# Inverse DFT over m written interleaved over four r, and a second buffer for x1s

## The chip, the cores and the metric

The kernel runs on one core of a Trainium2 chip. The metric is the device time of one execution in microseconds; lower is better. Before the change three runs took 784.08, 786.80 and 788.09 us, median 786.8.

## The reference

The computation has two parts. The first is a gated recurrence over time, the second a "Hyena" operator: a projection to three tensors, a long circular convolution of the second one through FFTs, a product of all three, and an output projection. Shapes: batch B = 4, time S = 6272, width D = 256, all float32.

```python
# first part: recurrence over t
sig = 1.0 / (1.0 + np.exp(-f_logit))
f = lower_bound + (1.0 - lower_bound) * sig
h = f[:, t] * h + (1.0 - f[:, t]) * x[:, t]        # for t in range(S); x becomes all h
# second part
proj = x @ w_proj                                   # (B, S, 3 D)
x1, x2, x3 = proj[..., :D], proj[..., D:2 * D], proj[..., 2 * D:]
X2 = np.fft.rfft(x2, n=S, axis=1)
H = np.fft.rfft(filter_fft, n=S, axis=0)[None]
x2_conv = np.fft.irfft(X2 * H, n=S, axis=1)
y = x1 * x2_conv * x3
return y @ w_out
```

## The kernel before

Time is split as t = 49 m + r with m from 0 to 127 and r from 0 to 48 (in the code Q = 49, M = 128), so that an FFT of length 6272 = 128 x 49 becomes matmuls over m and over r. One batch after the other goes through these phases:

- `hgrn(b)`: the recurrence, in 13 chunks of 512 time steps. A chunk loads x and f_logit, transposes them on TensorE (L146, L148), runs the scan on VectorE (L153), and computes x1 and x3 with float32 matmuls (L164). ScalarE copies x1 from PSUM into the tile `x1s` (L167), and VectorE multiplies x3 from PSUM with it into `z` = x1 * x3, float16 (L168). This runs twice per chunk, for jb = 0 and 1, the halves of the 256 channels. `x1s` has one buffer here, by `bufs=1`; the pool's own number is two. The scan's result also goes to `HA` for the later phases.
- `phase_p(b)`: projects x2 with weights read from `HA` at a step of 49 elements (L379) and evicts four r at a time into `x2` (L383 on VectorE, L385 on ScalarE), in runs of four float16.
- `phase_f1(b)`: the DFT over m (L394).
- `mini(b)` (L408 to L418) and `units(b)`: the DFT over r (L435), the product with the filter's spectrum (L439), the inverse over r (L447), evicted into `Th` (L450). `units(b)` is woven with `hgrn(b + 1)`.
- `phase_o(b)`: the inverse DFT over m, the gate and the output projection. It is the phase that the diff rewrites.

`phase_o` walks over r in 13 steps: twelve of four r and one with r = 48 alone. A step of four r has these instructions:

- L468, 16 matmuls on TensorE, each 64 contraction rows by 128 columns of m: for each r, two terms (`rr`) that accumulate, and two halves p of the channels, which use different 64 partitions of `Th` and write different PSUM banks. The result `pc` holds, for each p, four blocks of 128 m, one block per r.
- L473, one product on VectorE over 1024 elements per partition: `y` = `pc` * `z`, with y in float16 in the buffer `PP`. `z` lies in the order of time, so for a fixed r its elements over m are 49 elements (98 bytes) apart.
- L481, 16 matmuls on TensorE with y as the weights (128 x 128) and `w_out` as the moving operand (256 columns). `w_out` is split into a high and a low float16 part, `Woh` and `Wol`, and each weight tile is loaded for both.
- L485 evicts the result from PSUM to `osb` on ScalarE, and L486 stores it. `osb` has two buffers.

PSUM is one tile of eight banks, handed out in four pairs by `pair()`; `pc` takes one pair and the projection's result the next. The tile framework's scheduler sets the order of the instructions on each engine and adds the waits. On TensorE it puts two steps of `phase_o` together: 32 L468, then 32 L481, and so on, six times, and the single r = 48 at the end. The order on an engine is fixed when the program is built.

Of the kernel before, what the change touches and what calls it, by code (L numbers as in the profile page):

```python
# [9 lines left out]
F32 = mybir.dt.float32  # L10
# [3 lines left out]
AOP = mybir.AluOpType  # L14
# [10 lines left out]
Q = 49  # L25
TB = 98
CH = 512
# [17 lines left out]
def m0_of(r):  # L45
    return (128 * q_of(r) - r) // Q
# [22 lines left out]
def kernel(  # L69
# [10 lines left out]
    nc = tc.nc  # L80
# [32 lines left out]
    hg = ctx.enter_context(tc.tile_pool(name="hg", bufs=2))  # L113
    dram = ctx.enter_context(tc.tile_pool(name="dram", bufs=1, space=bass.MemoryType.DRAM))
    H = [dram.tile([TB, 2, UE * 64], F16, name=f"H{u}") for u in range(NU)]
    zt = [konst.tile([128, 2, S], F16, name="z0"), None]
# [4 lines left out]
    def pair():  # L121

        turn[0] = (turn[0] + 1) % turn[1]
        return PS[:, 2 * turn[0]:2 * turn[0] + 2]


    def hgrn(b):
        z = zt[b % 2]
        last = [None, None]
        for c in range(NCHK):  # L130
            t0 = c * CH
            nb = min(CH, S - t0) // 128
            n = nb * 128
            xt = hg.tile([128, 4, D], F32, name="xt", tag="xt", bufs=3)
            nc.sync.dma_start(xt[:, 0:nb], x[b, t0:t0 + n, :].rearrange("(j p) d -> p j d", p=128))
            ft = hg.tile([128, 4, D], F32, name="ft", tag="ft", bufs=3)
            nc.sync.dma_start(ft[:, 0:nb], f_logit[b, t0:t0 + n, :]
                              .rearrange("(j p) d -> p j d", p=128))
            nc.scalar.activation(ft[:, 0:nb], ft[:, 0:nb], AF.Sigmoid, scale=-1.0)  # L139
            nc.gpsimd.tensor_tensor(xt[:, 0:nb], xt[:, 0:nb], ft[:, 0:nb], op=AOP.mult)  # L140
            for kh in range(2):
                cols = slice(kh * 128, kh * 128 + 128)
                sT = PS[:, 6, 0:n]
                uT = PS[:, 7, 0:n]
                for j in range(nb):
                    nc.tensor.transpose(sT[:, j * 128:(j + 1) * 128], ft[:, j, cols], iden[:])  # L146
                for j in range(nb):
                    nc.tensor.transpose(uT[:, j * 128:(j + 1) * 128], xt[:, j, cols], iden[:])  # L148
                fT = hg.tile([128, CH], F32, name="fT", tag="fT")
                nc.scalar.activation(fT[:, 0:n], sT, AF.Identity,  # L150
                                     scale=nomc[:, kh:kh + 1], bias=1.0)
                h = hg.tile([128, CH], F32R, name="h", tag=f"h{kh}")
                nc.vector.tensor_tensor_scan(  # L153
                    h[:, 0:n], fT[:, 0:n], uT,
                    0.0 if c == 0 else last[kh][:, CH - 1:CH].bitcast(F32),
                    op0=AOP.mult, op1=AOP.add)
                last[kh] = h
                nc.gpsimd.tensor_copy(HA[:, HB[kh] + t0:HB[kh] + t0 + n],  # L158
                                      h[:, 0:n].bitcast(F32))
            for jb in range(2):  # L160
                for i in range(2):
                    js = slice(i * 256 + jb * 128, i * 256 + jb * 128 + 128)
                    for kh in range(2):
                        nc.tensor.matmul(PS[:, 4 + i, 0:n], W13[:, kh, js], last[kh][:, 0:n],  # L164
                                         start=(kh == 0), stop=(kh == 1))
                x1s = hg.tile([128, CH], F32, name="x1s", tag="x1s", bufs=1)
                nc.scalar.activation(x1s[:, 0:n], PS[:, 4, 0:n], AF.Copy, scale=ZS)  # L167
                nc.vector.tensor_tensor(z[:, jb, t0:t0 + n], PS[:, 5, 0:n], x1s[:, 0:n],  # L168
                                        op=AOP.mult)
            yield  # L170
# [282 lines left out]

    def phase_o(b):
        Th = st["Th"]
        z = zt[b % 2][:].rearrange("p k (m r) -> p k r m", r=Q)
        tf = Th[:].rearrange("p c g -> p (c g)")
        for r0 in range(0, Q, 4):
            rn = min(4, Q - r0)
            pc = pair()  # L460
            for i in range(rn):
                r = r0 + i
                sh = (128 - m0_of(r)) % 128
                for rr in range(2):
                    c0 = (rr * Q + r) * 128
                    for p in range(2):
                        ps = slice(64 * p, 64 * p + 64)
                        nc.tensor.matmul(pc[:, p, i * 128:(i + 1) * 128], tf[ps, c0:c0 + 128],  # L468
                                         ID[ps, rr, sh:sh + 128],
                                         start=(rr == 0), stop=(rr == 1))  # L470
            y = PP[:, r0 // 4 % 4 // 2, r0 // 4 % 2].rearrange(
                "p a i k -> p a (i k)").rearrange("p a (i m) -> p a i m", m=128)[:, :, 0:rn]
            nc.vector.tensor_tensor(  # L473
                y, pc[:, :, 0:rn * 128].rearrange("p a (i m) -> p a i m", m=128),
                z[:, :, r0:r0 + rn, :], op=AOP.mult)
            po = pair().rearrange("m a (q e) -> m (a q) e", e=256)
            for i in range(rn):
                n = 0
                for kh in range(2):
                    for w in (Woh, Wol):  # L480
                        nc.tensor.matmul(po[:, i, :], y[:, kh, i, :], w[:, kh, :],  # L481
                                         start=(n == 0), stop=(n == 3))
                        n += 1
            osb = cw.tile([128, 4, 256], F32, name="osb", tag="osb")
            nc.scalar.activation(osb[:, 0:rn, :], po[:, 0:rn, :], AF.Copy, scale=OS)  # L485
            nc.sync.dma_start(out[b].rearrange("(a r) d -> a r d", r=Q)[:, r0:r0 + rn, :],  # L486
                              osb[:, 0:rn, :])
            yield

    with tc.tile_pool(name="tmp", bufs=1) as tmp:  # L490
        prep = prepare(tmp)
        next(prep)
        weave((hgrn(0), NCHK), (prep, 1 + 13 + NU + 1))
# [6 lines left out]
    PP = cv.tile([128, 2, 2, 2, UE, 64], F16, name="PP")  # L500
    run(phase_p(0))
    run(phase_f1(0))
    for b in range(B):
        mini(b)
        if b + 1 < B:
            weave((units(b), NU), (hgrn(b + 1), NCHK))
        else:
            run(units(b))
        if b + 1 < B:
            wraps()  # L510
        run(phase_o(b))
        if b + 1 < B:
            run(phase_p(b + 1))
            run(phase_f1(b + 1))
# [30 lines left out]
```

## Time and profile before

| | |
|---|---|
| median of three runs | 786.8 us (784.08 to 788.09) |
| profiled execution, its own time | 786.94 us |
| its span | 785.2 us |
| mean granted TensorE clock | 0.954 |
| PE busy | 645.1 us (82%) |
| DVE busy | 567.9 us (72%) |
| ACT busy | 390.1 us (50%) |
| POOL busy | 198.4 us (25%) |
| HBM | 128 GB/s over the span |

PE is TensorE's matmuls, PEld its weight loads, DVE is VectorE, ACT ScalarE, POOL GpSimd, and SP issues the DMAs. A matmul's length in the profile includes its own pipeline, so matmuls overlap, and a busy PE isn't a PE at its peak. A group's line reads: line, engine, operation, output<-inputs, shapes, count, busy us, mean ns of one, idle time of the engine before them and what ended it. Line numbers are those of the kernel before, and the same in the kernel after.

### The profile page before, as it was taken

To read this page: it belongs to the slowest core of one execution; us is meant where nothing else is said; L and a number is where in the kernel's file an instruction comes from. 1 tells how busy PE (TensorE), PEld (TensorE's weight loads), DVE (VectorE), ACT (ScalarE), POOL (GpSimd) and SP (SyncE) were. 2 spreads that over 40 slices of the span, in tenths; PEclk is the share of its full clock that TensorE was granted. 3 is DMA by queue.
4 is the path that set the end of the run, shared out by engine and by line. 5 is a ranking of instruction groups with operands and counts; after the bars stand their busy time and mean duration, and the time that the engine had idled before them with its cause. 6 is when DMAs were issued, how large, how long until landed. Compare 5 with 4: busy or idle time off the path is not lost.

```text
span 785.2 us, 13221 instructions
## 1 busy us (share of the span) xinstructions
PE 645.1 (82%) x5252; PEld 483.2 (62%) x5252; DVE 567.9 (72%) x574; ACT 390.1 (50%) x495; POOL 198.4 (25%) x264
## 2 busy tenths in 40 slices
PE   4698897689999867889898766899999867989775
PEld 3576666575666555766665555766666656857554
DVE  6996464288888765697888566698898665889564
ACT  3697666475655423665455423665555223823232
POOL 2446434104454310005434400015443000001000
PEclk9899998899999989999999989999999999989899
DMA  9765546205664733224665723124663233012133
GB/s 326 242 213 153 184 128 203 97 1 174 193 186 156 256 127 134 88 66 137 196 191 158 236 108 153 70 70 149 213 194 122 89 148 157 13 51 83 59 140 141
DMA packets 73630, 113.99 MB, mean 145 GB/s; under 512 B 4416, under 2 KB 55488, under 8 KB 72800
## 3 DMA queue, kind: packets, MB, share of 16 engines
q1 hardware_dynamic: 73568, 113.15, 42.9%
q8 instruction: 41, 0.67, 0.4%
q14 instruction: 21, 0.17, 0.1%
HBM read 71.70 MB, written 28.90 MB: 128 GB/s over the span
## 4 chain that ended last, share of the span: by engine, by line
PE 36%; DVE 22%; issue 13%; ACT 8%; DMA 8%; POOL 0%; DVEq 0%; ACTq 0%; SPq 0%; POOLq 0%
PE PS L481 8%; DVE PP L473 8%; PE PS L164 7%; DVE h L153 7%; PE PS L379 5%; PE PS L447 5%; DVE PP L439 5%; DMA ft<-in_f_logit_dram 4%; DMA Hu<-H 4%; PE PS L468 2%; PE PS L394 2%; PE PS L148 2%; PE PS L346 2%; PE PS L435 2%; ACT x1s L167 1%
## 5 line engine op out<-in xcount | busy, mean ns | idle before, releaser
L473 DVE TENSOR_TENSOR PP<-PS,z 128x1024 f16<-128x1024 f32 (+1 forms) x52 | 113.4, 2220 | 76.0 <-PE PS L468 56.4
L164 PE MATMUL PS<-h,W 128*128 128x512 f32 (+1 forms) x416 | 148.9, 443 | 17.5 <-DVE h L153 10.7
L439 DVE TENSOR_TENSOR PP<-PS,Hu 98x1008 f16<-98x1008 f32 x128 | 151.2, 1194 | 9.6 <-PE PS L435 3.4
L481 PE MATMUL PS<-Woh,PP 128*128 128x256 f16 x392 | 101.8, 299 | 54.0 <-DVE PP L473 53.7
L140 POOL TENSOR_TENSOR xt<-xt,ft 128x1024 f32<-128x1024 f32 (+1 forms) x52 | 116.6, 2243 | 101.7 <-DMA xt<-in_x_dram 54.8
L153 DVE TENSOR_TENSOR_SCAN h<-fT,h,PS 128x512 fp32r<-128x512 f32 (+1 forms) x96 | 116.0, 1208 | 23.4 <-ACT fT L150 7.9
L481 PEld LDWEIGHTS <-PP 128*128 128x128 f16 x784 | 79.7, 106 | 78.9 <-DVE PP L473 63.4
L485 ACT ACTIVATE osb<-PS 128x1024 f32<-128x1024 f32 (+1 forms) x52 | 50.7, 975 | 139.6 <-PE PS L481 139.6
L168 DVE TENSOR_TENSOR z<-PS,x1s 128x512 f16<-128x512 f32 (+1 forms) x104 | 68.3, 657 | 59.2 <-ACT x1s L167 37.2
L447 PEld LDWEIGHTS <-PP 98*128 98x128 f16 x1024 | 84.7, 99 | 38.5 <-issue 28.2
L158 POOL CAST HA<-h 128x512 f16<-128x512 f32 (+1 forms) x104 | 61.6, 594 | 170.8 <-DVE h L153 167.6
L481 PE MATMUL PS<-Wol,PP 128*128 128x256 f16 x392 | 101.1, 297 | 0.0
L447 PE MATMUL PS<-VB,PP 98*128 98x196 f16 x512 | 95.6, 250 | 0.3
L164 PEld LDWEIGHTS PS<-h,W 128*128 128x128 f32 x416 | 66.2, 195 | 43.7 <-DVE h L153 24.6
L167 ACT ACTIVATE x1s<-PS 128x512 f32<-128x512 f32 (+1 forms) x104 | 59.3, 571 | 66.6 <-PE PS L164 62.9
L450 ACT CAST Th<-PS 128x784 f16<-128x784 f32 x64 | 51.9, 811 | 71.6 <-PE PS L447 71.5
L150 ACT ACTIVATE fT<-PS,nomc 128x512 f32<-128x512 f32 (+1 forms) x104 | 69.0, 663 | 33.8 <-PE PS L146 29.6
L435 PE MATMUL PS<-HA,FT 98*128 98x512 f16 x256 | 77.7, 386 | 4.6 <-DVE PP L439 2.8
L148 PE MATMUL PS<-iden,xt 128*128 128x128 f32 x392 | 67.9, 283 | 11.2 <-DVE h L153 10.2
L146 PE MATMUL PS<-iden,ft 128*128 128x128 f32 x392 | 70.2, 279 | 3.8 <-ACT fT L150 3.2
L139 ACT ACTIVATE ft<-ft 128x1024 f32<-128x1024 f32 (+1 forms) x52 | 52.4, 1008 | 29.7 <-DMA ft<-in_f_logit_dram 25.0
L447 PE MATMUL PS<-VA,PP 98*128 98x196 f16 x256 | 61.0, 250 | 4.5 <-ACT Th L450 2.5
(112 smaller groups left out, 792.3 us busy)
## 6 DMA issues: line engine op xcount, KB each, us to landing
xt<-in_x_dram SPq DMA_DIRECT2D x48, 512.0 KB
ft<-in_f_logit_dram SPq DMA_DIRECT2D x48, 512.0 KB
out_dram<-osb SPq DMA_DIRECT2D x48, 512.0 KB
Hu<-H SPq DMA_DIRECT2D x64, 196.0 KB
HA<-in_moe_filter_fft_dram SPq DMA_DIRECT2D x6, 1024.0 KB
HA<-HA SPq DMA_DIRECT2D x12, 512.0 KB
H<-HA SPq DMA_DIRECT2D x16, 196.0 KB
HA<-HA SPq DMA_DIRECT2D x4, 544.0 KB
```

Of the source, the lines that this page charges most:

```text
L140: nc.gpsimd.tensor_tensor(xt[:, 0:nb], xt[:, 0:nb], ft[:, 0:nb], op=AOP.mult)
L146: nc.tensor.transpose(sT[:, j * 128:(j + 1) * 128], ft[:, j, cols], iden[:])
L148: nc.tensor.transpose(uT[:, j * 128:(j + 1) * 128], xt[:, j, cols], iden[:])
L150: nc.scalar.activation(fT[:, 0:n], sT, AF.Identity, scale=nomc[:, kh:kh + 1], bias=1.0)
L153: nc.vector.tensor_tensor_scan(h[:, 0:n], fT[:, 0:n], uT, 0.0 if c == 0 else last[kh][:, CH - 1:CH].bitcast(F32), op0=AOP.mult, op1=AOP.add)
L164: nc.tensor.matmul(PS[:, 4 + i, 0:n], W13[:, kh, js], last[kh][:, 0:n], start=(kh == 0), stop=(kh == 1))
L168: nc.vector.tensor_tensor(z[:, jb, t0:t0 + n], PS[:, 5, 0:n], x1s[:, 0:n], op=AOP.mult)
L435: nc.tensor.matmul(PS[:, o, :], FT[:TB, tb, :], A[:TB, es, r, :], start=(n == 0), stop=(n == 1))
L439: nc.vector.tensor_tensor(P[:TB, o, :, :, 1:64], px.unsqueeze(1).broadcast_to([TB, 2, UE, 63]), hh, op=AOP.mult)
L447: nc.tensor.matmul(o, P[:TB, a, h, 2 * pr:2 * pr + 2, :], v[:TB], start=(n == 0), stop=(n == 3))
L473: nc.vector.tensor_tensor(y, pc[:, :, 0:rn * 128].rearrange("p a (i m) -> p a i m", m=128), z[:, :, r0:r0 + rn, :], op=AOP.mult)
L481: nc.tensor.matmul(po[:, i, :], y[:, kh, i, :], w[:, kh, :], start=(n == 0), stop=(n == 3))
```

## The change

Two edits. First, in `hgrn` the tile `x1s` gets the pool's two buffers instead of one. Second, in `phase_o` the order of the two inner indices m and i (the r within a step) is exchanged in `pc` and `y`: a matmul of L468 now writes every fourth word of its bank, so that the four r of one m lie side by side. L473 then reads `pc` and writes `y` in that order, and reads `z` in runs of four neighbours, a run every 49 elements. L481 takes the weights of one r out of `y` at a step of four elements. The number and the sizes of the instructions stay. For the last step (r = 48, rn = 1) nothing changes.

```diff
-                x1s = hg.tile([128, CH], F32, name="x1s", tag="x1s", bufs=1)
+                x1s = hg.tile([128, CH], F32, name="x1s", tag="x1s")
...
-        z = zt[b % 2][:].rearrange("p k (m r) -> p k r m", r=Q)
+        z = zt[b % 2][:].rearrange("p k (m r) -> p k m r", r=Q)
...
-                        nc.tensor.matmul(pc[:, p, i * 128:(i + 1) * 128], tf[ps, c0:c0 + 128],
+                        nc.tensor.matmul(pc[:, p, i:i + rn * 127 + 1:rn], tf[ps, c0:c0 + 128],
                                          ID[ps, rr, sh:sh + 128],
                                          start=(rr == 0), stop=(rr == 1))
-            y = PP[:, r0 // 4 % 4 // 2, r0 // 4 % 2].rearrange(
-                "p a i k -> p a (i k)").rearrange("p a (i m) -> p a i m", m=128)[:, :, 0:rn]
+            y = PP[:, r0 // 4 % 4 // 2, r0 // 4 % 2].rearrange("p a i k -> p a (i k)")
+            y = y[:, :, 0:rn * 128].rearrange("p a (m i) -> p a m i", i=rn)
             nc.vector.tensor_tensor(
-                y, pc[:, :, 0:rn * 128].rearrange("p a (i m) -> p a i m", m=128),
-                z[:, :, r0:r0 + rn, :], op=AOP.mult)
+                y, pc[:, :, 0:rn * 128].rearrange("p a (m i) -> p a m i", i=rn),
+                z[:, :, :, r0:r0 + rn], op=AOP.mult)
...
-                        nc.tensor.matmul(po[:, i, :], y[:, kh, i, :], w[:, kh, :],
+                        nc.tensor.matmul(po[:, i, :], y[:, kh, :, i], w[:, kh, :],
```

The second buffer of `x1s` changes the order in which the scheduler places instructions, in the setup (one exchange on ScalarE) and in the first weave, where `units` of batch 0 stands with `hgrn` of batch 1. On ScalarE (ACT), a place in that weave read before as follows; `fT` is the scan's factor, `ft` the gate's input, `Th` the output of `units`, and the bracket names the engines that an instruction waits for.

```order
L167 ACTIVATE x1s_1717<-PS_104 128x512 [waits PE_49]
L150 ACTIVATE fT_1767<-PS_104,nomc_66 128x512 [waits DVE_49,PE_49]
L139 ACTIVATE ft_1925<-ft_1925 128x1024 [waits DMAHW1_49]
L167 ACTIVATE x1s_1724<-PS_104 128x512 [waits DVE_49,PE_49]
L150 ACTIVATE fT_1780<-PS_104,nomc_66 128x512 [waits PE_49]
L450 CAST Th_1510<-PS_104 128x196x4 [waits PE_49]
```

In the changed kernel the same place on ScalarE reads:

```order
L167 ACTIVATE x1s_1717<-PS_104 128x512 [waits PE_49]
L150 ACTIVATE fT_1767<-PS_104,nomc_66 128x512 [waits DVE_49,PE_49]
L167 ACTIVATE x1s_1724<-PS_104 128x512 [waits PE_49]
L139 ACTIVATE ft_1925<-ft_1925 128x1024 [waits DMAHW1_49]
L150 ACTIVATE fT_1780<-PS_104,nomc_66 128x512 [waits DVE_49,PE_49]
L450 CAST Th_1510<-PS_104 128x196x4 [waits PE_49]
```

The second copy of x1 (`x1s_1724`) no longer waits for VectorE, and stands ahead of the sigmoid of a coming chunk (`ft_1925`).

On TensorE (PE) the first difference lies in the same weave, where L435 and L447 belong to `units` and L148 and L164 to `hgrn`:

```order
 L447 LDWEIGHTS PP
 L447 MATMUL PS<-VN,PP 128x196
+L435 LDWEIGHTS FT
+L435 MATMUL PS<-HA,FT 128x512
 L148 MATMUL PS<-iden,xt 128x128 x4
 L164 MATMUL PS<-h,W_73 128x512 x2
```

A matmul of `units` moves ahead of the transposes and projections of `hgrn`. The order of the two later weaves, of `phase_o` and of the phases between them is the same before and after on every engine.

## The prediction

> **What bounds the kernel now.** I read the page first, for the chain of work that ended last.
>
> ```profile
> span 785.2 us, 13221 instructions
> PE 36%; DVE 22%; issue 13%; ACT 8%; DMA 8%; POOL 0%; DVEq 0%; ACTq 0%; SPq 0%; POOLq 0%
> PE PS L481 8%; DVE PP L473 8%; PE PS L164 7%; DVE h L153 7%; PE PS L379 5%; PE PS L447 5%; DVE PP L439 5%; DMA ft<-in_f_logit_dram 4%; DMA Hu<-H 4%; PE PS L468 2%; PE PS L394 2%; PE PS L148 2%; PE PS L346 2%; PE PS L435 2%; ACT x1s L167 1%
> ```
>
> Three lines of `phase_o` (L481, L473, L468) hold about 18% of the chain, beside part of the "issue" share. Next, the busy time by stage for the four passes of `phase_o`; the columns are the stretch, its length, then busy time (instructions) of PE, PEld, DVE, ACT and POOL, granted clock, DMA share and GB/s.
>
> ```profile
> 275.50:321.70 46.20, 32.37 (x369) 25.12 (x368) 28.42 (x14) 12.30 (x12) 2.61 (x2) 0.91 0.32 128
> 450.80:498.00 47.20, 34.16 (x382) 26.20 (x379) 28.32 (x14) 12.30 (x12) 0.25 (x1) 0.89 0.31 125
> 619.70:666.00 46.30, 32.96 (x381) 25.51 (x381) 28.35 (x14) 12.30 (x12) 0.25 (x1) 0.93 0.31 127
> 735.00:785.20 50.20, 33.01 (x378) 25.24 (x372) 28.35 (x13) 12.68 (x13) 0.00 (x0) 0.90 0.32 129
> ```
>
> Together 189.9 us, and no engine is full: PE 33 of 47, DVE 28 of 47. So they take turns. The timeline of one period shows how: start, length, engine and line, and in brackets the idle time before.
>
> ```profile
> 466.41 1.07 PE L468 MATMUL PS<-ID,Th 64*128 64x128 f16 x32
> 466.56 1.02 ACT L485 ACTIVATE osb<-PS 128x1024 f32<-128x1024 f32 x1 [1.23 <-PE PS L481]
> 467.07 4.59 DVE L473 TENSOR_TENSOR PP<-PS,z 128x1024 f16<-128x1024 f32 x2 [2.58 <-PE PS L468]
> ...
> 469.47 1.64 PEld L481 LDWEIGHTS <-PP 128*128 128x128 f16 x16 [2.16 <-DVE PP L473]
> 469.47 0.28 PE L481 MATMUL PS<-Woh,PP 128*128 128x256 f16 x1 [1.99 <-DVE PP L473]
> ...
> 471.72 1.64 PEld L481 LDWEIGHTS <-PP 128*128 128x128 f16 x16 [0.61 <-DVE PP L473]
> ...
> 473.57 0.62 PE L468 MATMUL PS<-ID,Th 64*128 64x128 f16 x16
> ```
>
> One period is two steps of four r: 32 inverse-DFT matmuls (L468), two gate products on DVE (L473), two groups of 16 projection matmuls (L481). It lasts 473.57 - 466.41 = 7.16 us, and its path is 0.66 (first half of L468 until DVE starts) + 4.59 (both gate products) + 0.06 (hand-over, 471.72 against 471.66) + 1.85 (second L481 group until the next L468). TensorE stands idle for 2.16 + 0.61 us waiting for L473, so the gate sets the pace. Its price and the nearest rows, by shape:
>
> ```profile
> L473 DVE TENSOR_TENSOR PP<-PS,z 128x1024 f16<-128x1024 f32 x48 | 110.5, 2345 | 65.9 <-PE PS L468 46.3 <-issue 19.5
> L439 DVE TENSOR_TENSOR PP<-PS,Hu 98x1008 f16<-98x1008 f32 x128 | 151.2, 1194 | 9.6 <-PE PS L435 3.4 <-DMA Hu<-H 2.8 <-PE PS L447 2.3
> L383 DVE CAST x<-PS 128x1024 f16<-128x1024 f32 x24 | 34.6, 1440 | 21.9 <-PE PS L379 21.9
> L341 DVE CAST af<-PS 98x1024 fp32r<-98x1024 f32 x8 | 9.8, 1223 | 7.5 <-PE PS L334 7.5
> L325 DVE CAST f<-PS 128x1024 fp32r<-128x1024 f32 x6 | 7.4, 1233 | 0.6 <-PE PS L321 0.6
> ```
>
> L473 and L439 are the same operation on nearly as many elements; L439 reads runs of 63 and takes 1194 ns, L473 reads z one element in every 49 (98 bytes) and takes 2345. The step costs 1.1 ns per element.
>
> **The change, part by part.**
>
> *The gate reads z in runs of four.* 48 instructions. Without any price for runs it would come to L439's rate, 1024/1008 x 1194 = 1213 ns; if each run of four paid the step's 1.1 ns twice, 1213 + 256 x 2.2 = 1776. In between lies L383, which writes runs of four f16 at the same 98-byte step into x2: 1440 ns. That is the same geometry, so I take 1.44, that is 0.9 us off each L473. The four last steps of a pass (r = 48 alone) read z one by one as before: no gain.
>
> *What the shorter gate is worth.* In the period, the first gate product now ends at 0.66 + 1.44 = 2.10, the first L481 group starts at 2.16. A group starts its 16 matmuls 109 ns apart, from the chain of waits:
>
> ```profile
> 471.72 1.92 PE PS L481 x16
> ```
>
> (1.92 - 0.28 of the last one's own length)/15 = 0.109, so 1.75 us for a group. The second product ends at 0.66 + 2.88 = 3.54, before the first group is through at 3.91: it is hidden, and TensorE is late next. Period: 0.66 + 1.44 + 0.06 + 1.75 + 1.85 = 5.76, against 7.16: 1.40 saved. ACT's eviction of 1.02 us per step and the stores (DMA share 0.31 to 0.32 in the passes above) leave room.
>
> *The inverse DFT writes every fourth word of PSUM.* 768 of the 784 L468 matmuls.
>
> ```profile
> L468 PE MATMUL PS<-ID,Th 64*128 64x128 f16 x784 | 30.1, 225 | 7.4 <-ACT Th L450 6.0 <-ACT x1s L167 1.4
> ```
>
> 32 of them take 1.07 us and one about 0.22, so they start (1.07 - 0.22)/31 = 27.5 ns apart, since the two halves of 64 partitions run side by side: 55 ns per pair of 128 columns. No matmul of the trace writes PSUM with a step, so I bound it. Nothing: L325 and L341 are one copy with and without a 1 KB step between the words that it reads from PSUM, 1233 and 1223 ns. Much: L408 reads its moving operand at a 256-byte step.
>
> ```profile
> L408 PE MATMUL PS<-HA,FT 98*128 98x256 f16 x8 | 4.1, 601 | 0.4 <-DVE HA L398 0.4
> L379 PEld LDWEIGHTS <-HA 128*128 128x128 f16 x392 | 44.2, 144 | 8.1 <-DMA HA<-HA 5.4 <-issue 0.8
> L394 PEld LDWEIGHTS <-x 128*128 128x128 f16 x512 | 29.5, 98 | 10.9 <-ACT x L385 7.4 <-issue 2.4
> ```
>
> It takes 601 ns against 280 (the L481 of the timeline) for 256 columns, 1.25 ns more per column, so 160 ns per pair and 1.28 us per step. The stepped accesses of the trace cost a factor of 1.0 (L325), 1.45 (L379's weights at 98 bytes), 1.95 (L473) and 4 (L408, 321 more on 109 ns). I take 2, the factor of L473, whose step is also one element out of each neighbourhood: 55 ns more per pair, 8 x 55 = 0.45 us per step. Only the first step's share is on the path (the second runs under the first gate product, 1.97 against 2.55 us), so a period is 5.76 + 0.45 = 6.21.
>
> The Trainium skill ("PSUM — Partial Sum Buffer", Specifications) says that PSUM has 8-byte lines and that any access pattern that isn't contiguous slows matmuls significantly. By it, one fp32 per line instead of two is an estimate of half the write rate, 0.45 us per step and 761 us in all; by the row L325, whose step costs 10 ns in 1024, it would be 750. No run so far shows a stepped write.
>
> *The projection loads its weights at a step of four.* 768 loads. Between 98 ns (L394, no step) and 144 (L379, 98 bytes): up to 46 more, under the 109 ns from matmul to matmul, which covers it. Only a period's first load has no cover: 24 x 23 ns (the middle) = 0.5 us.
>
> *x1s gets a second buffer.* The waits that it can remove, with total, count and longest, and the wait around it:
>
> ```profile
> ACT x1s L167 <- DVE z L168: 3.8, 5, 1.5
> DVE z L168 <- ACT x1s L167: 37.2, 30, 5.0
> ```
>
> ACT waits 3.8 us for z's readers in all, and that is the ceiling. The 37.2 us stay: z still waits for its own x1s. After a product over jb = 0, L164 must refill bank 5 before the next product, so ACT's earlier copy mostly waits there instead. I take 1.0 us. The order changes only in the setup (one swap on ACT) and in the first weave (units of batch 0 with hgrn of batch 1); the two later weaves and all of `phase_o` stand as before. For the new order I allow the size of that ceiling, 4 us, either way, and nothing in the mean.
>
> *The clock.* Per pass, the first period and one later are longer.
>
> ```profile
> 290.08:298.41 8.33, 6.33 (x65) 4.65 (x64) 4.62 (x2) 2.05 (x2) 0.00 (x0) 0.80 0.37 153
> 466.41:473.57 7.16, 4.84 (x65) 3.87 (x64) 4.59 (x2) 2.05 (x2) 0.00 (x0) 1.00 0.35 145
> 185.00:272.00 87.00, 79.88 (x545) 55.39 (x542) 73.47 (x75) 47.33 (x71) 39.81 (x46) 1.00 0.58 185
> ...
> 734.27:743.01 8.74, 7.11 (x64) 5.39 (x64) 4.60 (x2) 1.02 (x1) 0.00 (x0) 0.61 0.01 2
> ```
>
> The granted clock falls there, to a mean of 0.80 in a later period and 0.61 in a first one. In the weave, with PE busy 92%, it is 1.00. A period now has TensorE waiting for 2.8 us of 7.16, then for 0.6 of 6.21 (L468 done at 1.97, L481 from 2.61), so I expect the later drop to vanish: those four periods come from 8.33 to 6.21. In a first period PE is behind the gate once the clock is down, so only the first product counts: 0.90 - 0.45 = 0.45.
>
> *The sum.* 24 periods: 16 x (7.16 - 6.21) = 15.2; 4 x (8.33 - 6.21) = 8.5; 4 x 0.45 = 1.8; x1s 1.0; weights -0.5. In all 26.0 us off the profiled execution's 786.94 (its span 785.2): 760.9. The median of the three runs, 786.8, is 0.1 lower, so 761.
>
> **The rivals.**
>
> *Stepped PSUM writes cost nothing.* For it: L325. Then 16 x 1.40 + 4 x (8.33 - 5.76) + 4 x 0.90 + 0.5 = 36.8, giving 750.
>
> *The inverse DFT becomes the bound.* The other side. At L408's price 32 L468 last 1.07 + 2.56 = 3.63, and both gate products hide under PE. The period is L468 + 1.75 + 1.85 = 7.23; it equals 7.16 at 1.245 us per step (156 ns more per pair, nearly four times as slow), and from there on the kernel gets slower. At 1.28 a usual period is 0.07 longer. If the clock drops stay, a period of 8.33 spends 8.33 - 0.66 - 2.35 - 0.06 = 5.26 from the first L481 on, and becomes 3.63 + 5.26 = 8.89, for eight periods 0.56 longer: 16 x 0.07 + 8 x 0.56 = 5.6, giving 793. Against it: a step of 16 bytes is smaller than L408's 256.
>
> *Runs of four aren't faster to read.* L383 shows runs on the write side only. With L473 at 2.35 and the writes at a factor of two, each period is 0.45 longer: 797. Against it: L473's price goes with its step, since L439 has none.
>
> *The clock still drops.* Four periods at 0.45 instead of 2.11: 768, inside the first case.
>
> **How the numbers follow.** About 0.5% (4 us) is what a measurement of this kernel tells from no change. My case with or without clock drops 0.50; free writes 0.28; the inverse DFT as the bound 0.10; runs no faster 0.06; the rest, 0.06, is a gain eaten in part by the first weave or by something that no row shows. Faster 0.82, same 0.08, slower 0.10. The range starts at 745 (free writes with a gate of 1213 ns: 750 - 24 x 0.23) and reaches 778 (768, plus 16 x 0.34 for a gate of 1776 ns, plus 4 for the order); both slower rivals stay outside, 0.16 in all.
>
> **What would show each step.** L473 near 1440 ns, and TensorE's idle time before L481 falling from 2.2 us to under 1; a period of 6.2 us; 32 L468 in 2.0 us instead of 1.07 (1.07 means free writes, 3.6 the bound); L481's loads at most 144 ns and its matmuls still 109 ns apart; no clock below 1.00 after a pass's first period; ACT's 3.8 us wait for L168 gone, the first weave within 4 us of before. I am wrong if L468's matmuls lie more than 100 ns apart, if L473 stays above 2 us, or if L481's matmuls move apart.

## The result and the profile after

The changed kernel takes 757.8 us (median of four runs, 752.8 to 762.2) against 787.4 before (the three runs and a fourth): the ratio is 0.9625, with a 95% interval from 0.9554 to 0.9696. The forecast was 761 us. The profiled execution took 752.78 us with a span of 751.1, so it lies 5 us under the median; the four runs go only roughly with their mean granted clock (752.78 us at 0.973, 756.37 at 0.956, 759.15 at 0.962, 762.17 at 0.951).

The chain of work that ended last, from the page of the changed kernel:

```profile
PE 45%; DVE 24%; issue 11%; ACT 10%; DMA 9%; POOL 1%; DVEq 0%; SPq 0%; ACTq 0%
PE PS L481 11%; PE PS L164 9%; DVE h L153 8%; PE PS L447 5%; PE PS L379 5%; DMA ft<-in_f_logit_dram 5%; DVE PP L439 4%; DVE PP L473 4%; PE PS L468 3%; PE PS L148 2%; DMA Hu<-H 2%; PE PS L435 2%; PE PS L346 2%; PE PS L394 2%; ACT x1s L167 2%
```

The gate (L473) has gone from 8% to 4%, and the TensorE lines beside it (L481, L468) carry more. The four passes of `phase_o`, by stage, with the columns as before:

```profile
278.66:315.47 36.81, 34.40 (x377) 30.98 (x374) 14.96 (x14) 12.32 (x12) 0.24 (x1) 0.98 0.39 158
444.11:480.73 36.62, 33.74 (x382) 30.53 (x379) 14.89 (x14) 12.32 (x12) 1.02 (x2) 1.00 0.41 165
602.71:639.34 36.63, 33.74 (x382) 30.52 (x379) 14.90 (x14) 12.32 (x12) 0.25 (x1) 1.00 0.39 159
710.91:751.10 40.19, 32.99 (x376) 29.67 (x370) 14.84 (x13) 12.71 (x13) 0.00 (x0) 1.00 0.40 161
```

They sum to 150.3 us, where before it was 189.8 (the passes cut at the same events): 39.5 us gained. DVE's busy time in a pass is halved, PE is nearly full, and the clock is at 0.98 to 1.00, where it was 0.89 to 0.93. The span became 34.1 us shorter, so 5.4 us were lost outside the passes. One usual period in the timeline:

```profile
461.04 1.92 PE L468 MATMUL PS<-ID,Th 64*128 64x128 f16 x32
461.19 1.02 ACT L485 ACTIVATE osb<-PS 128x1024 f32<-128x1024 f32 x1 [0.72 <-PE PS L481]
462.13 2.36 DVE L473 TENSOR_TENSOR PP<-PS,z 128x1024 f16<-128x1024 f32 x2 [3.63 <-PE PS L468]
...
463.41 3.42 PEld L481 LDWEIGHTS <-PP 128*128 128x128 f16 x32 [0.73 <-DVE PP L473]
463.41 0.30 PE L481 MATMUL PS<-Woh,PP 128*128 128x256 f16 x1 [0.45 <-DVE PP L473]
...
467.03 1.92 PE L468 MATMUL PS<-ID,Th 64*128 64x128 f16 x32
```

It lasts 5.99 us: 1.09 until the gate starts, 1.22 for the first product, 0.06 to hand over, and 3.62 for both L481 groups, which now follow each other without a wait. TensorE waits once, for 0.45 us. The groups by shape:

```profile
L473 DVE TENSOR_TENSOR PP<-PS,z 128x1024 f16<-128x1024 f32 x48 | 56.6, 1220 | 80.3 <-PE PS L468 65.1 <-issue 15.2
L468 PE MATMUL PS<-ID,Th 64*128 64x128 f16 x784 | 50.6, 313 | 7.1 <-ACT Th L450 7.1
L481 PEld LDWEIGHTS <-PP 128*128 128x128 f16 x784 | 83.4, 114 | 19.7 <-DVE PP L473 18.4
```

The gate is down from 2345 to 1220 ns. A matmul of the inverse DFT is up from 225 to 313 ns, and 32 of them take 1.92 us instead of 1.07, so that they start (1.92 - 0.31)/31 = 52 ns apart instead of 27.5. A weight load is up from 106 to 114 ns in the mean (from 98 to 114 where the clock is 1.00), and the L481 matmuls still start 109 ns apart.

### The profile page after: what moved, and what is told of

Its sections match the earlier page's. It is cut to its first block, busy times and chain, and to the rows that moved or that the text cites. A ratio compares the mean times of both kernels' runs of the same rounds, so it can differ in the third digit from the quotient of the medians.

```text
span 751.1 us, 13229 instructions
## 1 busy us (share of the span) xinstructions
PE 650.6 (87%) x5252; PEld 503.8 (67%) x5252; DVE 514.1 (68%) x574; ACT 390.4 (52%) x495; POOL 197.6 (26%) x264
## 4 chain that ended last, share of the span: by engine, by line
PE 45%; DVE 24%; issue 11%; ACT 10%; DMA 9%; POOL 1%; DVEq 0%; SPq 0%; ACTq 0%
PE PS L481 11%; PE PS L164 9%; DVE h L153 8%; PE PS L447 5%; PE PS L379 5%; DMA ft<-in_f_logit_dram 5%; DVE PP L439 4%; DVE PP L473 4%; PE PS L468 3%; PE PS L148 2%; DMA Hu<-H 2%; PE PS L435 2%; PE PS L346 2%; PE PS L394 2%; ACT x1s L167 2%
## 5 line engine op out<-in xcount | busy, mean ns | idle before, releaser
L164 PE MATMUL PS<-h,W 128*128 128x512 f32 (+1 forms) x416 | 148.5, 441 | 16.6 <-DVE h L153 10.1
L473 DVE TENSOR_TENSOR PP<-PS,z 128x1024 f16<-128x1024 f32 (+1 forms) x52 | 59.5, 1182 | 91.8 <-PE PS L468 76.6
L168 DVE TENSOR_TENSOR z<-PS,x1s 128x512 f16<-128x512 f32 (+1 forms) x104 | 68.4, 658 | 67.4 <-ACT x1s L167 39.9
L447 PEld LDWEIGHTS <-PP 98*128 98x128 f16 x1024 | 86.4, 100 | 40.9 <-issue 29.5
L481 PE MATMUL PS<-Woh,PP 128*128 128x256 f16 x392 | 87.9, 275 | 11.8 <-DVE PP L473 11.4
L447 PE MATMUL PS<-VB,PP 98*128 98x196 f16 x512 | 97.7, 254 | 0.4 <-DVE PP L439 0.3
L481 PEld LDWEIGHTS <-PP 128*128 128x128 f16 x784 | 83.4, 114 | 19.7 <-DVE PP L473 18.4
L167 ACT ACTIVATE x1s<-PS 128x512 f32<-128x512 f32 (+1 forms) x104 | 59.4, 572 | 69.6 <-PE PS L164 68.7
L164 PEld LDWEIGHTS PS<-h,W 128*128 128x128 f32 x416 | 65.9, 195 | 43.2 <-DVE h L153 23.8
L481 PE MATMUL PS<-Wol,PP 128*128 128x256 f16 x392 | 87.2, 273 | 0.0
L435 PE MATMUL PS<-HA,FT 98*128 98x512 f16 x256 | 78.0, 388 | 4.8 <-DVE PP L439 3.0
L148 PE MATMUL PS<-iden,xt 128*128 128x128 f32 x392 | 68.0, 281 | 12.0 <-DVE h L153 11.0
L148 PEld LDWEIGHTS PS<-iden,xt 128*128 128x128 f32 x392 | 46.2, 142 | 30.4 <-DVE h L153 24.2
```

The source lines that it names most:

```text
L435: nc.tensor.matmul(PS[:, o, :], FT[:TB, tb, :], A[:TB, es, r, :], start=(n == 0), stop=(n == 1))
L447: nc.tensor.matmul(o, P[:TB, a, h, 2 * pr:2 * pr + 2, :], v[:TB], start=(n == 0), stop=(n == 3))
L473: nc.vector.tensor_tensor(y, pc[:, :, 0:rn * 128].rearrange("p a (m i) -> p a m i", i=rn), z[:, :, :, r0:r0 + rn], op=AOP.mult)
L481: nc.tensor.matmul(po[:, i, :], y[:, kh, :, i], w[:, kh, :], start=(n == 0), stop=(n == 3))
```

## The experiments

My theory after the result: the gain is the shorter gate, less a price for the stepped PSUM writes; the second buffer of x1s does nothing; and the clock stays up because TensorE waits less.

**One edit at a time.** The first run takes the interleaving without the second buffer:

```diff
-                x1s = hg.tile([128, CH], F32, name="x1s", tag="x1s")
+                x1s = hg.tile([128, CH], F32, name="x1s", tag="x1s", bufs=1)
```

> The interleaving alone, with one buffer for x1s; every engine then has the order of before. My theory: all of the gain comes from phase_o, so L473 takes 1.22 us, 32 L468 take 1.92 us, a period 5.99 us, and the time is that of the changed kernel or up to 3 us less (its first weave ended 3.1 us later than before): 754 to 758 us. Rival: the second buffer of x1s carries part of the gain, and without it the time is 761 us or more.

Measured: 753.3 us, just under the 754 to 758 that I expected, ratio 0.9566 (0.9528 to 0.9604), L473 at 1219 ns, a period of 5.99 us. As the theory had it, the interleaving alone has the whole gain. It is no slower than both edits together (0.9554 to 0.9696; the two intervals overlap). The first gate starts 278.2 us after the span's start with the old order of the first weave, and 278.7 with the new one. So the 3 us that the changed kernel's profile lost ahead of its first pass (275.5 before) can come without the new order.

The second takes the kernel before with the second buffer alone (the first pair of lines of the diff of the change).

> The second buffer for x1s alone; every engine then has the order of the changed kernel, phase_o is that of before. My theory: a period stays at 7.16 us, the clock still drops in each pass, ACT's 3.8 us wait for L168 goes and nothing ends sooner by it: 784 to 790 us. Rival 1: the new order of the first weave costs, the first gate starts 3 us later, 790 us. Rival 2: the buffer helps in all four weaves with hgrn, 783 us or less.

Measured: 789.1 us against 786.1, ratio 1.0022 (0.9997 to 1.0046), L473 at 2346 ns. The waits in this run:

```profile
ACT x1s L167 <- PE PS L164: 68.7, 58, 3.0
DVE z L168 <- ACT x1s L167: 38.4, 27, 5.4
```

The wait of ACT for L168 (3.8 us before) is gone from the list. ACT now waits for TensorE instead (62.9 us before, 68.7 now), and z's wait for x1s has stayed (37.2 and 38.4). So the buffer removes a wait that nobody was held up by. Its gain is nothing, or a loss of up to half a per cent; the rival with a gain is out. The other rival, a cost of the new order, stays open: in this profile the first gate starts at 281.1 us, 5.6 later than before, but the 3.0 us of the whole aren't clear of noise.

**The stepped PSUM writes alone.** The kernel before with these lines; z, y and the weights stay as they were:

```diff
-                        nc.tensor.matmul(pc[:, p, i * 128:(i + 1) * 128], tf[ps, c0:c0 + 128],
+                        nc.tensor.matmul(pc[:, p, i:i + rn * 127 + 1:rn], tf[ps, c0:c0 + 128],
...
-                y, pc[:, :, 0:rn * 128].rearrange("p a (i m) -> p a i m", m=128),
+                y, pc[:, :, 0:rn * 128].rearrange("p a (m i) -> p a i m", i=rn),
```

> The kernel before, with L468 writing every fourth word of PSUM and the gate reading PSUM at that step; z is still read one element in 49, y and the weights are as before. My theory: 32 L468 take 1.92 us instead of 1.07, L473 stays at 2.35 us because its price is z's step, a period is 0.43 us longer (7.59), and the time is 793 to 798 us, the less the clock drops the lower. Rival: the layout of pc or y makes the gate fast, L473 falls below 2 us and the time below 780.

Measured: 792.7 us, ratio 1.0074 (1.0042 to 1.0106). The groups and a later period of this run:

```profile
L473 DVE TENSOR_TENSOR PP<-PS,z 128x1024 f16<-128x1024 f32 x48 | 110.4, 2341 | 71.2 <-PE PS L468 50.9 <-issue 20.3
L468 PE MATMUL PS<-ID,Th 64*128 64x128 f16 x784 | 51.9, 321 | 5.5 <-ACT Th L450 4.5 <-ACT x1s L167 1.1
```

```profile
461.64:469.24 7.60, 5.64 (x70) 4.56 (x66) 4.59 (x3) 1.96 (x2) 0.00 (x0) 1.00 0.35 142
```

L473 kept its 2.34 us though PSUM was read at a step, so the price of the gate before was z's step. The writes slow L468 by themselves, and a period is 7.60 us, 0.43 longer. The time is just under the 793 to 798 us that I expected: the later clock drop of each pass is gone here too. By the rows of its matmuls, TensorE waits 1.6 + 0.3 us of 7.6 here, where it was 2.0 + 0.3 of 7.2.

**Runs of four without the stepped writes.** The changed kernel, but with L468 writing blocks and DVE doing the stepping:

```diff
-                        nc.tensor.matmul(pc[:, p, i:i + rn * 127 + 1:rn], tf[ps, c0:c0 + 128],
+                        nc.tensor.matmul(pc[:, p, i * 128:(i + 1) * 128], tf[ps, c0:c0 + 128],
...
-                y, pc[:, :, 0:rn * 128].rearrange("p a (m i) -> p a m i", i=rn),
+                y, pc[:, :, 0:rn * 128].rearrange("p a (i m) -> p a m i", i=rn),
```

> The changed kernel, but L468 writes each r as a block of 128 words as before, and the gate reads PSUM at a step of 128 words; z in runs of four, y interleaved. My theory: a step between words read from PSUM costs DVE nothing, so L473 stays at 1.22 us, 32 L468 take 1.07 us again, a period is 0.66 + 1.22 + 0.06 + 3.62 = 5.56 us, and the time is 10 us below the changed kernel, 747 us. Rival: DVE pays for the step in PSUM, L473 takes 1.44 us or more, a period is 5.8 us or more and the time within 5 us of the changed kernel.

Measured: 745.1 us, ratio 0.9469 (0.9421 to 0.9518). The groups of this run and a usual period:

```profile
L473 DVE TENSOR_TENSOR PP<-PS,z 128x1024 f16<-128x1024 f32 x48 | 56.5, 1219 | 75.1 <-PE PS L468 52.9 <-issue 22.1
L468 PE MATMUL PS<-ID,Th 64*128 64x128 f16 x784 | 30.0, 224 | 9.3 <-ACT Th L450 9.3
```

```profile
458.11:463.68 5.57, 4.70 (x72) 4.33 (x68) 2.36 (x3) 2.06 (x3) 0.00 (x0) 1.00 0.54 218
```

All three numbers are those of the theory: the gate keeps 1.22 us while it reads PSUM at a step of 512 bytes, L468 is back at 224 ns, and a period is 5.57 us. So the changed kernel paid for its interleaving on the engine where a step in PSUM costs something, and the same order is free for the engine that reads the bank. Against the interleaving alone, timed in the same series, this run is 8 us shorter.

The same kernel with one buffer for x1s:

> The kernel whose gate steps through PSUM, with one buffer for x1s as before the change. My theory: the second buffer gains nothing and its order costs up to 3 us, so this is 742 to 746 us, the same as with two buffers or a little below. Rival: the second buffer gains where phase_o is short, and the time is 748 us or more.

Measured: 744.0 us, ratio 0.9453 (0.9413 to 0.9492). The second buffer makes no difference here either. In all three pairs the kernel with two buffers has the longer median (by 3.0, 4.5 and 1.1 us, the last two from runs of different series), but no pair is clear of noise.

**Runs of two.** Pairs of r side by side; two products of 512 elements per step (against the changed kernel, shortened):

```diff
-  pc[:, p, i:i + rn * 127 + 1:rn]
+  pc[:, p, (i // 2) * 256 + i % 2:(i // 2) * 256 + i % 2 + min(rn, 2) * 127 + 1:min(rn, 2)]
...
-  y, pc[...], z[:, :, :, r0:r0 + rn]
+  y[h], pc[... the 256 words of pair h ...], z[:, :, :, r0 + 2 * h:r0 + 2 * h + w2]     # h = 0, 1
```

> One buffer for x1s; L468 writes every second word, pairs of r side by side, and the gate is two products of 512 elements per step, each reading z in runs of two. For the prices alone. Writes: if any step leaves half of a place unused, every second word costs the same as every fourth (matmuls 52 ns apart instead of 27.5, about 311 ns long); the rival is a price that grows with the step, 27.5 to 40 ns apart. Reads of z: 512 elements with no step take 0.69 us (L168). If each place visited costs a fixed extra (1.1 ns), a product takes 0.69 + 256 x 1.1 ns = 0.97 us; if two elements per place are enough to hide it, 0.69 us.

The timeline follows. This kernel has 16 matmuls of the inverse DFT and 16 of the projection in turn, so the time of its one run, 753.3 us, isn't compared:

```profile
461.58 1.05 PE L468 MATMUL PS<-ID,Th 64*128 64x128 f16 x16
461.91 1.52 DVE L477 TENSOR_TENSOR PP<-PS,z 128x512 f16<-128x512 f32 x2 [1.52 <-PE PS L468]
```

16 matmuls in 1.05 us, one lasting 317 ns in the mean: (1.05 - 0.32)/15 = 49 ns apart, about the 52 of every fourth word. The write price hardly grows from a step of two words to one of four, as the first theory had it. A product of 512 took 799 ns in the mean. That is 111 more than L168's 688 without a step, and 0.17 less than the 0.97 us of a fixed extra per place: neither reading fits exactly, and I leave open how the extra splits.

**Whether TensorE's waiting drops the clock.** The kernel with one x1s buffer and the gate stepping through PSUM, with the gate's instruction written twice in a row:

> The kernel with the gate stepping through PSUM and one buffer for x1s, and each gate product issued twice (the same result written twice), so that TensorE waits about as long as in the kernel before although z is read in runs of four. Theory on the clock: it falls when TensorE waits for too much of a period. A period is 0.66 + 4 x 1.18 + 0.06 + 1.85 = 7.3 us, TensorE waits for 2.9 us of it as before, and a later period of each pass falls to a mean clock of 0.80 again; 788 to 793 us. Rival: the drops come with the reading of z one by one, or with the length of the pass; then no period after a pass's first one has a clock below 1.00, and the time is 786 us or less.

Measured: 819.9 us, ratio 1.0429 (1.0381 to 1.0477), well above my number. The timeline shows where I was off, and two periods show the clock:

```profile
488.57 2.35 DVE L473 TENSOR_TENSOR PP<-PS,z 128x1024 f16<-128x1024 f32 x2 [4.88 <-PE PS L468]
490.84 2.35 DVE L476 TENSOR_TENSOR PP<-PS,z 128x1024 f16<-128x1024 f32 x2
492.11 3.42 PEld L484 LDWEIGHTS <-PP 128*128 128x128 f16 x32 [3.31 <-DVE PP L476]
```

```profile
469.58:479.07 9.49, 6.28 (x68) 4.84 (x64) 4.62 (x4) 1.93 (x3) 0.00 (x0) 0.82 0.32 131
488.57:496.40 7.83, 4.69 (x72) 4.33 (x68) 4.62 (x5) 2.05 (x3) 0.00 (x0) 1.00 0.23 92
```

The scheduler put the copies behind both first products (two L473, then two L476), so TensorE waits once for 3.1 us instead of twice. A usual period is 7.83 us instead of the 7.3 expected, or 9.49 with a clock of 0.82, and 12 of the 20 periods after the first of each pass fall to 0.81 or 0.82; 4 of 20 did in the profile before. The longer period 24 times (about 13 us) and eight more drops of 1.66 us (13 us) make up most of the miss, by my estimate.

On the question, the run decides for the first theory: z is read in runs of four here, and the drops are back and more frequent. Nor is it the length of a pass: with the stepped writes alone a period is 7.60 us, longer than before, and none of the 20 drops. None does either in the kernels whose TensorE waits 0.45 us (the changed one) or 0.9 us (the gate stepping through PSUM) in a usual period. Such a count is rough, as it comes from one profile: the run with the second buffer alone, whose `phase_o` is that of before, has 2 of 20. Whether the share of idle time or the length of a single wait decides isn't separated: drops came with waits of 2.0 and 3.1 us, none with 1.6 us or less.

**A faster version.** With the gate at 1.22 us, what is left is the order in which TensorE waits for the gate of its own step. In this run `phase_o` issues the inverse DFT two steps ahead (blocks in PSUM, one x1s buffer; shortened):

```diff
+        pcs = [idft(r0) for r0 in steps[:2]]        # idft: the L468 matmuls of one step
+        for k, r0 in enumerate(steps):
+            ...                                      # the gate of step k, from pcs[k]
+            if k + 2 < len(steps):
+                pcs.append(idft(steps[k + 2]))
+            ...                                      # projection, eviction and store of step k
```

> One buffer for x1s, blocks of 128 words in PSUM, z in runs of four, and in phase_o the inverse DFT is written two steps ahead of its projection, so that TensorE alternates 16 L468 of a later step with 16 L481. My theory: TensorE then never waits for the gate; two steps take 2 x (16 x 27.5 ns + 16 x 109 ns + two changes of 0.2 us) = 5.2 us or less against 5.56, 9 to 15 us less in all, 730 to 737 us. Rival: the eviction on ACT and the stores of 1 MB per two steps become the bound, two steps stay at 5.5 us or more and the time above 740 us.

Measured: 726.6 us, ratio 0.9231 (0.9201 to 0.9261). Its timeline (L470, L481, L491 and L495 are here the inverse DFT, the gate, the projection and the eviction):

```profile
444.47 0.62 PE L470 MATMUL PS<-ID,Th 64*128 64x128 f16 x16
444.62 1.03 ACT L495 ACTIVATE osb<-PS 128x1024 f32<-128x1024 f32 x1 [1.45 <-PE PS L491]
445.02 1.67 PEld L491 LDWEIGHTS <-PP 128*128 128x128 f16 x16
445.13 1.23 DVE L481 TENSOR_TENSOR PP<-PS,z 128x1024 f16<-128x1024 f32 x1 [1.20 <-PE PS L470]
446.89 0.45 PEld L470 LDWEIGHTS <-Th 64*128 64x128 f16 x16 [0.20 <-issue]
...
449.32 0.62 PE L470 MATMUL PS<-ID,Th 64*128 64x128 f16 x16
```

Two steps take 449.32 - 444.47 = 4.85 us, the gate runs wholly beside TensorE, and neither the eviction nor the stores have become the bound. It is the fastest version, 17 us under the same kernel without the reordering (744.0), and below the range that I gave for it (730 to 737): two steps were to take up to 5.2 us. With 27.5 and 109 ns per matmul, each change between the two kinds of matmul takes about 0.12 us by the measured 4.85, where I had counted 0.2.

## Why the prediction came out right

The total was 3 us off and the direction right. By its steps:

- **The gate in runs of four: right in kind, too dear.** I took 1440 ns from L383, which writes runs of four; measured 1220, at the lower end of 1213. Runs of four at a 98-byte step cost next to nothing to read here, and the rival that they aren't faster is out. What makes L383 slower than its neighbours doesn't carry over from writing to reading. It is 0.22 us per period, 5 us in all.
- **The stepped PSUM writes: right.** A factor of two was taken, 0.45 us per step; 27.5 ns became 52, a factor of 1.9, and the gate starts 0.43 us later. The Trainium skill's rule ("PSUM — Partial Sum Buffer", Specifications: 8-byte lines, patterns that aren't contiguous slow matmuls) agrees with the runs, as the price is nearly the same at a step of two words (49 ns apart) and of four (52). The rival that the writes are free is out, and so is that of the inverse DFT as the bound.
- **DVE's side of PSUM: right, and not followed up.** The bound from L325 against L341 said that a step in PSUM costs DVE nothing. The prediction used it only as an end of the range for TensorE's writes; it also meant that the interleaving needed no stepped write at all. Without one the kernel takes 745.1 us, against 753.3 for the interleaving alone in the same series and 757.8 for the changed kernel.
- **The weights at a step of four: right.** A load takes 114 ns, within the 98 to 144 of the prediction, and the cover holds: the matmuls stay 109 ns apart, and two groups of L481 take 3.62 us.
- **The period: 6.21 forecast, 5.99 measured,** the difference being the gate. The 16 usual periods, among them three that end a pass and were shortened more (6.84 to 5.23 us), gained about 20 us instead of 15.2. The four with a clock drop gained 9.8 instead of 8.5.
- **The clock: the later drops went, as expected, so that rival is out, but the first periods were undersized.** I counted 1.8 us for them, as if the drop there stayed. The four first periods (from the pass's first gate to the next period's):

```profile
278.66:284.92 6.26, 6.26 (x64) 5.59 (x62) 2.45 (x3) 2.05 (x2) 0.00 (x0) 0.87 0.16 63
444.11:450.15 6.04, 5.59 (x69) 5.12 (x67) 2.35 (x2) 2.05 (x2) 0.77 (x1) 1.00 0.24 94
602.71:608.76 6.05, 5.60 (x69) 5.13 (x67) 2.36 (x3) 2.05 (x2) 0.00 (x0) 1.00 0.15 64
710.91:716.96 6.05, 5.54 (x70) 5.07 (x66) 2.36 (x2) 2.05 (x2) 0.00 (x0) 1.00 0.16 66
```

  They sum to 24.4 us. Before they were 8.03, 9.12, 8.30 and 8.61, at a clock of 0.60 to 0.79: 34.1, so the gain is 9.7 us. That is one profile. With the interleaving alone, the first two still had a clock of 0.68 and 0.84 (7.86 and 6.56 us), and with the gate stepping through PSUM three of the four lay between 0.65 and 0.76. What comes ahead of a pass may have its part in them; this wasn't settled.
- **x1s: 1.0 us forecast, no gain measured.** The reason stood in the same paragraph (z waits for its own x1s and for L164), and should have led to nothing.
- **What the sum left out.** The passes gained 39.5 us where the terms had 25: 20 instead of 15.2, 9.8 instead of 8.5, and 9.7 instead of 1.8, as above. Outside them the profiled execution lost 5.4 us: 3.1 ahead of the first pass, and 2.5 between the third pass and the last, where the last batch's projection, DFT, `mini` and `units` run alone:

```profile
639.34:710.91 71.57, 63.90 (x566) 49.23 (x565) 56.54 (x50) 30.99 (x32) 3.94 (x16) 0.93 0.16 50
```

  Before, this stage took 69.03 us at a clock of 0.95. Neither could be tied to an edit: over the profiles of the runs above, the first gate starts between 274.3 and 278.4 us with the old order of the first weave, and between 277.9 and 281.1 with the new one. Nor does the clock of that stretch settle it: it was 0.95 both at 275.5 (before) and at 278.7 (after), and 0.93 at 278.1 (the gate twice) and at 281.1 (the second buffer alone). So a median within 3 us of the forecast is partly luck: the passes gained 14 us more than the terms, and the median lies about 10 us above what the passes of the profile alone would give.
- **The chances don't fit the rivals.** The two slower rivals forecast 793 and 797 us, both more than the 4 us that the prediction took as noise, and had 0.16 together; "slower" was given 0.10.

## What to carry to other kernels

When two layouts of one tensor meet in PSUM, let the reader do the stepping: here DVE took the same 1.22 us when it read PSUM at a step of 512 bytes, while stepped writes put TensorE's matmuls 1.9 times as far apart. When an elementwise product sits on the path, first look at the step of its SBUF operand: runs of four instead of single elements nearly halved it (2345 to 1220 ns). And a wait that is listed isn't a wait that counts: ask what releases next after it, as with x1s.

## What the runs showed of the hardware

- A product of 1024 elements took 2345 ns with one float16 operand at a 98-byte step, 1220 ns with that operand in runs of four at the same step, and a product of 512 took 799 ns with runs of two. The 1220 ns stayed (1219) when PSUM was read at a step of 512 bytes.
- L468's matmuls started 27.5 ns apart with contiguous output, 49 at a step of two words and 52 at four.
- By the rows of its matmuls, TensorE waited 2.0 + 0.3 us in a usual period of 7.2 us before; the granted clock fell in 4 of the 20 periods after a pass's first one, and in 2 of 20 with the second buffer alone. At 3.1 of 7.8 it fell in 12 of 20. It fell in none of 20 at 1.6 + 0.3 of 7.6 (the stepped writes alone), at 0.45 of 6.0 (the changed kernel) and at 0.9 of 5.6 (the gate stepping through PSUM). Each count is of one profile.
